# Attention with eight wide products per unit: two bunches of four in place of one per four value products

## Chip, cores and metric

The kernel runs on one core of one Trainium2 chip. The metric is the time of one execution on the device, in microseconds. It is the median of several runs.

## What is computed

Attention (batch 4, 8 heads, 576 positions, head size 64) in float32: heads 0 to 3 see the last 32 positions, heads 4 to 7 every fourth of the last 128. The result, 2304 rows of 512, goes to one of eight experts per row (the arg max of a normalised product with the experts' embeddings), and then through a dense layer pair of 2048 columns. The core of it:

```python
scores = scale * np.matmul(q, k.transpose(0, 1, 3, 2))
scores = np.where(masks[None], scores, -1e9)
attn = np.exp(scores - np.max(scores, axis=-1, keepdims=True))
attn = attn / (np.sum(attn, axis=-1, keepdims=True) + 1e-09)
x = np.matmul(attn, v)                      # attention
expert_idx = np.argmax(logits, axis=1)      # one expert per row
out[mask] = gate_w[mask, None] * (np.maximum(x[mask] @ w1[e], 0) @ w2[e])
h = x @ w_in
return (h - np.tanh(h)) @ w_out
```

## The kernel before

The attention is cut into 19 units. A unit holds 128 query positions in four slots of 64 columns for each of two halves (`par`: partitions 0 to 63 and 64 to 127). Kinds are `d` (dilated heads, with positions four apart brought together), `p` (plain heads) and two for the ends of the sequences (`l`, `t`). Within a unit each group of 32 queries sees 64 keys, so all products of scores and values are small: 64 rows by 32 columns of TensorE's array. They are float32, and each shows in the trace as two records.

The order of the work is written out by hand. The loop over n issues, on each engine in this order:

- loads of later units on SP's queue (`plan[n]`; the first load waits for the copy of pT of the unit before);
- `scores(n + 2)`: two mask products into the score tile `sc` (one buffer, two banks; columns 0 to 255 of each are used), four transposes of keys of unit n + 3, 32 score products' records, four transposes of queries, 32 more (L641, L550, L651);
- `softmax(n + 2)`: on VectorE the maximum (L664) and the difference (L667, which frees `sc`), on ScalarE the exponential (L672);
- `mid[n]`: parts of the routing of earlier rows;
- `values(n)`: into the tile `xo` (one buffer, two banks), 32 value products (64 records, L719), with a wide product of 240 columns ahead of each four products (L717, which calls L631); then four transposes of the probabilities of unit n + 1 (L680), which ScalarE copies to `pT` (L683). VectorE then forms the reciprocal of the sums (L728, L730) and scales (L739, which frees `xo`);
- `after[n]`: copies of values into place (L504, L510, mostly VectorE) and the routing (norm, split, transposes by DMA, choice of expert, scatter of rows to the experts' places by GpSimd).

The wide product, `busy(o)`, multiplies the scaled unit matrix by 16 columns of the mask, repeated, into columns of a bank that nobody reads. It computes nothing that is used. The helper records it at L631.

After unit 16's values the last rows are read back by SP (`load_xt`), a clearing copy writes zeros behind the first expert's rows (`load_first`, L824), and the scatters of the last rows follow on GpSimd. When all rows have been written, the experts begin (L1345), and then the dense layers (L1540, L1596).

Of the kernel before, what the change touches and what calls it, by code (L numbers as in the profile page):

```python
# [56 lines left out]
def kernel(  # L57
# [336 lines left out]
    with ExitStack() as actx:  # L394
# [187 lines left out]
        def run(steps):  # L582
            for f in steps:
                f()
# [6 lines left out]
        def key_window(n, s, g):  # L591
            kind, b, c = units[n]
            if kind == "d":
                return kTd[c][:, s, W * g:W * g + 2 * W]
            if kind == "p":
                o = 256 * c + 128 * (s // 2) + W * g
                return kTp[:, s % 2, o:o + 2 * W]
            if kind == "l":
                return kTl[c][:, g, s, :]
            return kTt[:, s % 2, 2 * (s // 2) + g // 2, W * (g % 2):W * (g % 2) + 2 * W]  # L600

        def value_window(n, s, g):
            kind, b, c = units[n]
            if kind == "d":
                return vwd[b % 2][:, g, c, s, :]
            if kind == "p":
                return vwp[b % 2][:, 4 * (2 * c + s // 2) + g, s % 2, :]
            if kind == "l":
                return vwl[:, g, c, s, :]
            return vwt[:, 2 * (s // 2) + g // 2, g % 2, s % 2, :]  # L610

        def mask_of(n):

            kind, _, c = units[n]
            if kind == "p" and not c:
                return mask_sb[:, :, :]
            e = 0 if kind == "d" else 2
            return mask_sb[:, e].unsqueeze(1).to_broadcast([128, 4, 2 * W])
# [9 lines left out]
        def busy(o):  # L628


            nc.tensor.matmul(  # L631
                o.rearrange("p (r j) -> p r j", j=16), lhsT=idm[:],
                rhs=mask_sb[:, 0, 0:16].unsqueeze(1).to_broadcast([128, o.shape[1] // 16, 16]),
                start=True, stop=True, skip_group_check=True,
            )

        def scores(n, between=(), tag="sc"):
            between = list(between)
            sc = ps.tile([128, 2, 512], F32, tag=tag, name="sc", bufs=1)
            for par in range(2):  # L640
                nc.tensor.matmul(  # L641
                    sc[:, par, 0:256].rearrange("p (r j) -> p r j", r=4), lhsT=idm[:], rhs=mask_of(n),
                    start=True, stop=False, skip_group_check=True,
                )
            half = len(between) // 2
            for par in range(2):
                p0 = 64 * par
                run(between[half * par:half * par + half])
                for s in range(4):
                    for g in range(4):  # L650
                        nc.tensor.matmul(  # L651
                            sc[32 * g:32 * g + 32, par, 64 * s:64 * s + 64],
                            lhsT=qT[n][p0:p0 + 64, s, W * g:W * g + W],
                            rhs=key_window(n, s, g)[p0:p0 + 64],
                            start=False, stop=(s == 3), skip_group_check=True,
                        )
            return sc
# [51 lines left out]
        def values(n, between=()):  # L709
            kind, b, cp = units[n]  # L710
            between = list(between)
            pT = pTs.pop(n)
            xo = ps.tile([128, 2, 512], F32, tag="xo", name="xo", bufs=1)
            for par in range(2):
                p0 = 64 * par
                for s in range(4):
                    busy(xo[:, par, 272:512])  # L717
                    for g in range(4):
                        nc.tensor.matmul(  # L719
                            xo[32 * g:32 * g + 32, par, 66 * s:66 * s + D + 1],  # L720
                            lhsT=pT[p0:p0 + 64, s, 32 * g:32 * g + 32],
                            rhs=value_window(n, s, g)[p0:p0 + 64],
                            start=True, stop=True, skip_group_check=True,
                        )
            run(between)
            xv = xo[:, :, 0:264].rearrange("p a (s d) -> p a s d", d=66)
            rd = wk.tile([128, 2, 4], F32, tag="rd", name="rd")
            nc.vector.tensor_scalar(out=rd, in0=xv[:, :, :, D], scalar1=1e-9, scalar2=None, op0=ALU.add)  # L728
            rr = wk.tile([128, 2, 4], F32, tag="rr", name="rr")
            nc.vector.reciprocal(out=rr, in_=rd)  # L730
            if kind == "p":
                o = xp[b][:, 0, 2 * cp:2 * cp + 2].rearrange("p t (h a d) -> p a (t h) d", h=2, a=2)
            elif kind == "t":
                o = xp[B][:, 0].rearrange("p t (h a d) -> p a (t h) d", h=2, a=2)
            else:
                if cp == 0:
                    xdt[kind, b] = tp.tile([128, 4, 4, D], F32, tag="xd", name="xd")
                o = xdt[kind, b][:, 2 * cp:2 * cp + 2]
            nc.vector.tensor_tensor(  # L739
                out=o, in0=xv[:, :, :, 0:D], in1=rr.unsqueeze(3).to_broadcast([128, 2, 4, D]), op=ALU.mult  # L740
            )
            if kind == "d" and cp == 1:
                (nc.gpsimd if b < 3 else nc.sync).dma_start(out=xd_d[b, 0:128, :], in_=xdt[kind, b].rearrange("p c h d -> p (c h d)"))
            if kind == "l" and cp == 1:
                nc.sync.dma_start(out=xl_d, in_=xdt[kind, b].rearrange("p c h d -> p (c h d)"))
# [409 lines left out]
        init_p()  # L1155
        run(transpose_qk(0))
        softmax(0, scores(0, transpose_qk(1)))
        for g in range(4):
            expand_v(0, g, slice(0, 1))
        softmax(1, scores(1, transpose_qk(2), "xo"))  # L1160
        for g in range(2):
            expand_v(0, g, slice(1, 2))
        mid[0] += [(expand_v, (0, g, slice(1, 2))) for g in range(2, 4)]
        run(transpose_p(0))
        for n in range(N):
            pace["ins"] = done["ins"]
            for f, a in plan[n]:
                f(*a)
            if n + 2 < N:
                softmax(n + 2, scores(n + 2, transpose_qk(n + 3) if n + 3 < N else ()))  # L1170
            for f, a in mid[n]:
                f(*a)
            values(n, transpose_p(n + 1) if n + 1 < N else ())
            for f, a in after[n]:
                f(*a)
            if n == 14:
                dctx.close()
                late.append(actx.enter_context(tc.tile_pool(name="late", bufs=1, side="right")))
# [588 lines left out]
```

## Time and profile before

| | |
|---|---|
| median of three runs | 810.5 us (807.91 to 811.0) |
| profiled execution | 816.94 us, span 815.3 us |
| mean granted clock of TensorE in it | 0.912 |
| TensorE matmul busy | 773.1 us (95%) |
| VectorE busy | 483.1 us (59%) |
| ScalarE busy | 382.0 us (47%) |
| GpSimd busy | 197.9 us (24%) |

The attention lies in the first 182 us of the span, the rest of the routing up to about 209 us, experts and dense layers behind it. PE is TensorE's matmuls, PEld its weight loads, DVE VectorE, ACT ScalarE, POOL GpSimd, SP the engine that issues most DMAs. The granted clock (PEclk) is 1.00 at 2.4 GHz and 0.50 at 1.2 GHz. Matmuls are pipelined, so the time between the starts of two is what one costs, and the busy time of one is longer. A row of the view by windows gives, for a stretch: its length, then the busy time (and count) of PE, PEld, DVE, ACT and POOL, then the granted clock, the busy share of the 16 DMA engines, and GB/s. A row of the timeline gives start, duration, engine, line, operation, output and inputs, shapes, the number of instructions merged, and in brackets the idle time before and what ended it.

### The profile page before, as it was taken

Reading aid. Unit: us, or ns where it says so; the run is one execution under the profiler, and the core shown is the slowest. Engines: PE = TensorE matmul, PEld = TensorE weight load, DVE = VectorE, ACT = ScalarE, POOL = GpSimd, SP = SyncE. Lnnn points to the kernel's source line nnn. Section 1 sums busy time; section 2 is a strip of 40 time slices with the busy share of each in tenths; the row PEclk is TensorE's granted clock in tenths of the full one; section 3 lists DMA queues with packets and bytes.
Section 4 is the critical chain, followed back from the end, with each engine's and each line's share of the span. In section 5 each row is a group of like instructions: output and inputs, shape, how many; then the busy total and the mean of one; then the engine's idle time right before and its main releaser. Section 6 shows DMA issues by size and latency. Waiting matters only on the chain.

```text
span 815.3 us, 16969 instructions
## 1 busy us (share of the span) xinstructions
PE 773.1 (95%) x6773; PEld 470.5 (58%) x6773; DVE 483.1 (59%) x1019; ACT 382.0 (47%) x812; POOL 197.9 (24%) x244
## 2 busy tenths in 40 slices
PE   8999999994799999999999899999999999999994
PEld 4666666562466666688885455555555555555541
DVE  4679465447578777889878999534334343343430
ACT  5446445324365565667765666523423333333401
POOL 2036252407600000000002222322322321321321
PEclk9898575555799999999999999999999999999998
DMA  9768773455898896899840240100100000000001
GB/s 220 164 161 178 119 183 97 84 168 212 260 258 232 244 251 213 203 287 266 283 161 26 29 130 1 39 1 0 39 1 1 29 12 1 17 22 1 9 34 42
DMA packets 115828, 95.33 MB, mean 117 GB/s; under 512 B 72187, under 2 KB 99099, under 8 KB 115739
## 3 DMA queue, kind: packets, MB, share of 16 engines
q1 hardware_dynamic: 109083, 77.12, 35.5%
q0 software_dynamic: 5312, 16.40, 6.1%
q8 instruction: 55, 0.90, 0.5%
q10 hardware_dynamic: 1344, 0.62, 0.3%
q14 instruction: 34, 0.28, 0.1%
HBM read 67.12 MB, written 18.26 MB: 105 GB/s over the span
## 4 chain that ended last, share of the span: by engine, by line
PE 58%; DVE 5%; issue 4%; DMA 3%; ACT 3%; POOL 1%; POOLq 0%; ACTq 0%; SPq 0%; DVEq 0%
PE hp L1540 21%; PE po L1596 19%; PE ph L1345 9%; PE y L1365 8%; DMA wst<-in_moe_w 2%; DVE w2l L187 1%; ACT w2h L177 1%; POOL out L1605 1%; DMA xTe<-xs 1%; DVE hl L1354 1%; DVE y L1424 1%; ACT sq L1403 0%; DVE x2l L1430 0%; POOL gl L1578 0%; ACT u L1550 0%
## 5 line engine op out<-in xcount | busy, mean ns | idle before, releaser
L1553 DVE CUSTOM_DVE_ANT_0 U<-u,sig 128x384 f32<-128x384 f32 x96 | 52.1, 580 | 161.1 <-ACT u L1550 161.1
L1578 POOL TENSOR_TENSOR gl<-c,gh 128x768 f16<-128x768 f32 x48 | 82.5, 1720 | 260.0 <-ACT gh L1577 260.0
L1540 PE MATMUL hp<-x2h,win_h 128*128 128x384 f16 x384 | 125.8, 328 | 4.6 <-DVE c L1560 4.2
L1550 ACT ACTIVATE u<-hp 128x384 f32<-128x384 f32 x96 | 46.0, 485 | 176.1 <-PE hp L1540 170.4
L1540 PE MATMUL hp<-x2h,win_l 128*128 128x384 f16 x384 | 125.8, 328 | 0.0
L1540 PE MATMUL hp<-x2l,win_h 128*128 128x384 f16 x384 | 124.6, 327 | 0.0
L1345 PE MATMUL ph<-xTe,w1h 128*128 128x352 f16 (+6 forms) x512 | 103.4, 296 | 10.9 <-DMA xTe<-xs 8.5
L1540 PEld LDWEIGHTS <-win_h 128*128 128x128 f16 x768 | 75.5, 98 | 58.6 <-DVE c L1560 6.0
L1596 PE MATMUL po<-wo_h,gl 128*128 128x512 f16 x288 | 109.2, 379 | 0.0
L1596 PE MATMUL po<-wo_h,gh 128*128 128x512 f16 x288 | 109.2, 379 | 0.0
L1596 PE MATMUL po<-wo_l,gh 128*128 128x512 f16 x288 | 109.2, 379 | 0.0
L1596 PEld LDWEIGHTS <-gh 128*128 128x128 f16 x576 | 56.3, 98 | 64.5 <-issue 1.0
L1345 PE MATMUL ph<-xTe,w1l 128*128 128x352 f16 (+6 forms) x256 | 75.7, 296 | 0.0
L1365 PE MATMUL y<-hh,w2h 128*128 128x352 f16 (+6 forms) x256 | 74.7, 292 | 0.0
L1365 PE MATMUL y<-hh,w2l 128*128 128x352 f16 (+6 forms) x256 | 74.6, 291 | 0.0
L1365 PE MATMUL y<-hl,w2h 128*128 128x352 f16 (+6 forms) x256 | 74.6, 291 | 0.0
L1345 PEld LDWEIGHTS <-w1h 128*128 128x128 f16 x512 | 50.7, 99 | 26.2 <-issue 9.5
L1365 PEld LDWEIGHTS <-w2h 128*128 128x128 f16 x512 | 50.1, 98 | 17.1 <-issue 0.8
L1540 PEld LDWEIGHTS <-win_l 128*128 128x128 f16 x384 | 37.7, 98 | 26.7 <-issue 0.3
L1582 DVE SCALAR_TENSOR_TENSOR c<-U,c 128x768 f32<-128x768 f32 x48 | 46.0, 958 | 11.2 <-ACT U L1572 11.2
L631 PE MATMUL xo<-mask_sb,idm 128*128 128x240 f16 x152 | 49.6, 326 | 0.0
L1596 PEld LDWEIGHTS <-gl 128*128 128x128 f16 x288 | 28.2, 98 | 34.0
(277 smaller groups left out, 1287.0 us busy)
## 6 DMA issues: line engine op xcount, KB each, us to landing
wst<-in_moe_w SPq DMA_DIRECT2D x64, 512.0 KB, 7.1
wst<-in_moe_w_in SPq DMA_DIRECT2D x16, 512.0 KB, 6.6
wst<-in_moe_w_out SPq DMA_DIRECT2D x16, 512.0 KB, 4.1
vwp<-in_v SPq DMA_DIRECT2D x16, 144.0 KB, 5.2
rv<-in_v SPq DMA_DIRECT2D x4, 512.0 KB, 5.3
rk<-in_k SPq DMA_DIRECT2D x16, 128.0 KB, 4.7
rq<-in_q SPq DMA_DIRECT2D x16, 128.0 KB, 3.3
xp<-xd_d SPq DMA_DIRECT2D x4, 512.0 KB, 5.7
```

Of the source, the lines that this page charges most:

```text
L177: nc.scalar.activation(out=hi, in_=st, func=ACTF.Copy, scale=SW)
L187: nc.vector.scalar_tensor_tensor(out=lo, in0=st, scalar=SW, in1=hi, op0=ALU.mult, op1=ALU.subtract)
L631: nc.tensor.matmul(o.rearrange("p (r j) -> p r j", j=16), lhsT=idm[:], rhs=mask_sb[:, 0, 0:16].unsqueeze(1).to_broadcast([128, o.shape[1] ...
L1345: nc.tensor.matmul(ph[:, 0:CAPS[e]], lhsT=wt[e, f // 2][w][:, c:c + 128], rhs=xT[:, a + d, 0:CAPS[e]], start=(i == 0), stop=(i == 11), ski ...
L1354: rest.append(lambda: nc.vector.scalar_tensor_tensor(out=hl[:, f, c], in0=ph[:, c], scalar=0.0, in1=hh[:, f, c], op0=ALU.max, op1=ALU.subtract
L1365: nc.tensor.matmul(y[dc][:, 0:CAPS[e]], lhsT=w[:, c:c + 128], rhs=h[:, f, 0:CAPS[e]], start=(f == 0 and i == 0), stop=(f == 7 and i == 2), ...
L1540: early(b, "x2", nc.tensor.matmul(hp[:, a, 0:NB], lhsT=w[d][:, 128 * f:128 * f + 128], rhs=x[d][:, c0:c0 + NB], start=(w is win_h and x is ...
L1550: nc.scalar.activation(out=u[:, a], in_=hv[:, a], func=ACTF.Square, accum_out=usum[:, n:n + 1])
L1553: early(b, "sg", nc.vector.tensor_tensor_reduce(out=U[:, a], in0=u[:, a], in1=sig2[:, c0:c0 + NB], scale=1.0, scalar=0.0, op0=ALU.mult, op ...
L1578: nc.gpsimd.tensor_tensor(out=gl, in0=tc_, in1=gh, op=ALU.subtract)
L1582: nc.vector.scalar_tensor_tensor(out=c, in0=U, scalar=T0, in1=c, op0=ALU.add, op1=ALU.mult)
L1596: nc.tensor.matmul(po[t][:], lhsT=g[:, a, 128 * t:128 * t + 128], rhs=w, start=(f == 0 and i == 0), stop=(f == 15 and i == 2), skip_group_ ...
```

## The change

In `scores()` four wide products stand ahead of the two masks, in columns 256 to 495 of the score tile's two banks in turn. In `values()` four stand ahead of all value products, in columns 272 to 511 of `xo`'s two banks in turn, and the one ahead of each four value products is gone. A unit has eight wide products of 240 columns, as before.

```diff
         def scores(n, between=(), tag="sc"):
             between = list(between)
             sc = ps.tile([128, 2, 512], F32, tag=tag, name="sc", bufs=1)
+            for i in range(4):
+                busy(sc[:, i % 2, 256:496])
             for par in range(2):
...
             xo = ps.tile([128, 2, 512], F32, tag="xo", name="xo", bufs=1)
+            for i in range(4):
+                busy(xo[:, i % 2, 272:512])
             for par in range(2):
                 p0 = 64 * par
                 for s in range(4):
-                    busy(xo[:, par, 272:512])
                     for g in range(4):
```

## Rows read from the trace of the kernel before

**Rows 1.** The page: granted clock of TensorE in 40 slices, in tenths.
```profile
PEclk9898575555799999999999999999999999999998
```

**Rows 2.** Windows: the stage of 15 units, then two stretches at the lower clock.
```profile
24.23:157.09 132.86, 131.73 (x2363) 85.86 (x2362) 85.07 (x200) 63.59 (x124) 48.09 (x74) 0.72 0.64 144
...
74.89:112.44 37.55, 37.31 (x548) 24.12 (x548) 20.25 (x58) 16.84 (x33) 16.71 (x26) 0.50 0.81 178
...
132.92:182.00 49.08, 49.08 (x725) 29.95 (x724) 22.73 (x80) 20.04 (x41) 15.58 (x26) 0.50 0.48 127
```

**Rows 3.** Windows of single units; sums of the seven heavy and the eight light.
```profile
32.17:38.81 6.64, 6.64 (x152) 4.45 (x150) 5.11 (x10) 2.93 (x5) 1.74 (x2) 1.00 0.64 181
...
67.67:75.13 7.46, 6.82 (x150) 4.41 (x151) 7.16 (x12) 3.90 (x8) 5.57 (x6) 0.98 1.26 181
...
146.21:157.09 10.88, 10.88 (x151) 6.69 (x150) 5.81 (x20) 4.91 (x11) 1.88 (x5) 0.50 0.45 86
sum 61.51, PE 60.38 PEld 39.69 DVE 46.66 ACT 30.39 POOL 24.47; mean PE 8.63 PEld 5.67 DVE 6.67 ACT 4.34 POOL 3.50
...
sum 71.35, PE 71.35 PEld 46.17 DVE 38.41 ACT 33.19 POOL 23.62; mean PE 8.92 PEld 5.77 DVE 4.80 ACT 4.15 POOL 2.95
```

**Rows 4.** Timeline of TensorE in a unit at the lower clock.
```profile
101.83 1.08 PE L651 MATMUL sc<-kTd,qT 64*32 64x64 f32 x32
102.84 0.38 PE L631 MATMUL xo<-mask_sb,idm 128*128 128x240 f16 x1
103.15 0.44 PE L719 MATMUL xo<-vwd,pT 64*32 64x65 f32 x8
...
108.33 1.12 PE L680 MATMUL pt<-id,pr 128*128 128x128 f32 x4
109.24 0.63 PE L641 MATMUL sc<-mask_sb,idm 128*128 128x256 f16 x2
109.67 1.06 PE L550 MATMUL tr<-id,rk 128*128 128x128 f32 x4
```

**Rows 5.** The same at the upper clock.
```profile
113.19 0.28 PE L631 MATMUL xo<-mask_sb,idm 128*128 128x240 f16 x1
...
116.84 0.66 PE L680 MATMUL pt<-id,pr 128*128 128x128 f32 x4
117.34 0.38 PE L641 MATMUL sc<-mask_sb,idm 128*128 128x256 f16 x2
117.55 0.60 PE L550 MATMUL tr<-id,lk 128*128 128x128 f32 x4
...
119.25 0.65 PE L651 MATMUL sc<-kTp,qT 64*32 64x64 f32 x32
119.83 0.28 PE L631 MATMUL xo<-mask_sb,idm 128*128 128x240 f16 x1
```

**Rows 6.** Groups of instructions in 24.23 to 157.09 us: busy us, mean ns, idle before.
```profile
L950 PE MATMUL rps<-en,xT 128*128 128x8 f16 x96 | 2.9, 169 | 0.0
```

**Rows 7.** Timeline of TensorE around the first values().
```profile
18.84 0.32 PE L719 MATMUL xo<-vwd,pT 64*32 64x65 f32 x8 [0.97 <-ACT pT L683]
...
23.32 1.12 PE L680 MATMUL pt<-id,pr 128*128 128x128 f32 x4
```

**Rows 8.** Timeline of TensorE, SP's queue and GpSimd behind unit 16's scores.
```profile
159.13 0.38 PE L631 MATMUL xo<-mask_sb,idm 128*128 128x240 f16 x1
...
172.47 0.39 SPq L824 DMA_DIRECT2D xs<-z  x1
...
181.32 1.09 POOL L1061 DMA_INDIRECT xs<-xg,ri  x1 [18.81 <-DMA xs<-z]
```

**Rows 9.** The masks' line: its weight loads, ns min/median/max, first and last start.
```profile
L641 PEld LDWEIGHTS <-idm x38: 95/104/152, 6.9 to 157.1; 128*128 128x128 f16 x38
```

**Rows 10.** Windows: the transfers of 20 to 120 us.
```profile
20.00:120.00 100.00, 98.87 (x1837) 64.46 (x1830) 67.55 (x144) 48.26 (x94) 37.46 (x56) 0.76 0.74 161
```

## The prediction

> **What bounds the kernel now.** I began with the page: the granted clock is near full everywhere except in slices 4 to 11, the second part of the attention stage [rows 1]. So I then cut that stage by clock. In 24.2 to 157.1 us the mean granted clock is 0.72: between the two levels, 2.4 and 1.2 GHz, that is 44% of the time at the upper and 56% at the lower, and TensorE is busy for 131.7 of 132.9 us [rows 2]. TensorE's own queue is the limit in this stage, and the level of its clock sets the pace.
>
> Third, the stage by unit. It holds 15 units, each from one pair of masks to the next. A unit wholly at the upper clock takes 6.64 us, one at the lower 10.88 us, and TensorE is busy throughout both [rows 3]. Seven of the units carry so much VectorE work (46.66 us together, 6.7 each) that it would be next: in one of them VectorE is busy for 7.16 of 7.46 us, and TensorE already idle for 0.64. The other eight hold 38.41 us, 4.8 each [rows 3].
>
> Fourth, the inside of a unit on TensorE. At the lower clock a wide product and its four value products (each shows as two records, hence x8) take 0.69 us from wide to wide, and eight such groups 5.49 us, from 102.84 to 108.33. Of that, 0.31 us pass from the start of a wide product to the first value product. But 32 score records of the same small tiles, in an unbroken row, take 1.01 us, and two masks, as wide products as these, 0.43 us [rows 4]. At the upper clock eight groups take 3.65 us, 32 score records 0.58 us and two masks 0.21 us [rows 5]. So eight wide products cost 8 x 0.11 = 0.9 us and 64 small records 2 x 0.58 = 1.2 us when each kind runs in a row, 2.1 us, but 3.65 us when they alternate. The remaining 1.5 us are 16 changes between wide and small tiles.
>
> **What the change does, part by part.** It removes and adds no wide product: eight per unit before and after. It moves four of them out of values() ahead of the masks in scores(), and puts the other four ahead of all value products.
>
> *values(), upper clock.* Four wide products at 0.105 (half a mask pair) are 0.42 us, the one change to small tiles 0.10 (0.31 less 0.21 at the lower clock, taken alike), 64 small records 2 x 0.58 = 1.16: 1.68 us for 3.65. *Lower clock:* 4 x 0.215 + 0.10 + 2 x 1.01 = 2.98 us for 5.49.
>
> *scores().* Four wide products more: 0.42 or 0.86 us. They go ahead of the masks with the same weights, so no change of tile is added. Net, a unit loses 3.65 - 1.68 - 0.42 = 1.55 us at the upper clock and 1.65 us at the lower: 6.64 becomes 5.1 and 10.85 becomes 9.2. This is from both ends: 0, if the alternation is not what costs, to these 1.6 us. I take the upper end, since scores and masks are the nearest rows and have the same shapes.
>
> *Waits.* The first wide product of scores() now waits for the score tile (VectorE's L667 of the unit before), where the mask did; masks, transposes and scores are behind it as before. In the seven heavy units that wait will be there each time, and the 0.42 us come after it; VectorE's own copies (L510, L504) cover them, and without that cover they are in the terms above. In values() the wide products wait for the xo tile only, and run before pT has come. No DMA and no instruction of another engine moves within its queue, on SP and POOL neither.
>
> *What is late next.* With TensorE at 5.1 us, VectorE sets the heavy units: 46.66 x 7.46/7.16 = 48.6 us. The light ones are 8 x 5.1 = 40.8 us. Four units carry the router's small products too (L950 alone 2.9 us, the smaller ones estimated at 0.9, at the lower clock; half at the upper) [rows 6]: 1.9 us. The whole stage at the upper clock would take 91.3 us for 132.9.
>
> *The clock.* Where the level rose, at 112.4 us, TensorE had come through masks, transposes and scores, and the alternating value part followed [rows 2, 4, 5]. The alternation keeps the array waiting at 16 changes per unit, of which the bunches leave two, and the same products then fill less time. That speaks for more of the upper level. Against it, in the heavy units TensorE will stand idle for 1.8 us (6.9 less 5.1) ahead of the scores: the unit with 0.64 us idle ends at 75.1 us, and the level fell at 74.9 [rows 2, 3]. I let half of the seven heavy units fall, and one and a half light ones that follow them before it rises: 5 of 15. They cost 3.5 x (9.2 - 6.9) + 1.5 x (9.2 - 5.1) = 14.2 us more: 91.3 + 14.2 = 105.5, a saving of 27 us. The ends are none low (41.5 us saved) and ten low (seven heavy and three light: 91.3 + 16.1 + 12.3 = 119.7, 13 us saved).
>
> *Start.* The first values() runs from 18.84 to 23.32 us, 4.5 us at a falling clock [rows 7]. Its value products alone are 1.3 us, since its wide products can go before pT is there; less three times 0.42 us ahead of the first scores: 2 us saved (0 to 3).
>
> *Tail.* values(16) begins at 159.13 us at the lower clock; the clearing copy that follows its result through the DRAM copy of the rows is issued at 172.47 and GpSimd waits 18.81 us for it until 181.32, and all scatters that the experts' rows need come behind it [rows 8]. This chain moves as a whole with the end of values(16): 5.49 - 2.98 = 2.5 us (3.8 at the upper clock). values(17) and (18) lie beside it and give nothing.
>
> Sum: 27 + 2 + 2.5 = 31.5 us off the profiled execution's own 816.9 us (span 815.3): **785 us**. The median of the three runs is 810.5, 6.4 us less. If the three had more of the upper clock in this stage, the changed kernel has no further 6 us to gain; if the difference is elsewhere, it is 779. I stay with 785.
>
> On the weight loads, rows and skill differ. Every wide product has its own load of 95 to 104 ns, the masks too, and yet a pair of masks takes 0.21 us at the upper clock and twice that, 0.43, at the lower [rows 4, 5, 9]: the pair's time goes with the clock alone, so the second load is hidden. The Trainium skill ("TensorE: Matmul & The Clock Gate", Part 3, "The mechanism") says that a weight load runs beside a matmul only when their row groups differ, and all wide products have the same. By it, each of the bunch would show its load; that is the first rival below.
>
> **The rivals.**
>
> *1. The wide products of a bunch show their loads.* 8 x 0.096 = 0.77 us per unit, so a unit keeps half its saving. On 16 units 12 us, less what VectorE's work hides in the heavy ones (an estimate: a third): 8 us, 793 us. The spacing of the masks speaks against it. Chance 0.08.
>
> *2. The loads become the bound.* In 20 to 120 us the DMA engines are busy 74% of the time [rows 10]. By the sum above this stretch would take some 78 us (its share of the 27, and the 2 of the start), with the same transfers: 95%. If the engines hold no more than 80% in the mean, it takes 92: 8 us saved, and 8 in the rest of the stage, with the tail 18.5 in all: 798 us. For it: one unit shows 1.26 for its transfers already (more than the engines can hold at once). Against it: TensorE is busy through that stretch, so at today's pace the loads are in time [rows 3, 10]. Chance 0.15.
>
> *3. Slower: the clock stays at the lower level through the whole stage.* Its place is the wait ahead of the scores: one idle time per unit in the heavy ones, and 64 small records with no wide product between them in all. Price: 15 x 9.2 + 3.8 (router's products at that clock) = 141.8 us, 9 more than now, less 2.5 in the tail, and nothing at the start: 823 us. It decides from about 14 of 15 units at the lower clock on; today it is 56%. Against it: the total of TensorE work per unit is the same in less time. The Trainium skill (same page, "A second HAM failure mode") tells of a kernel whose micro-idle times between groups of matmuls made the clock go to and fro; by that rule this rival is the likelier one, and the idle time before 74.9 us agrees with it, while the full use of TensorE in the light units does not. Chance 0.05.
>
> *4. It does not do what it says:* the groups cost the same in a row, and the clock keeps its share: 810 to 817 us. The rows of scores and masks speak against it. Chance 0.05.
>
> **How the numbers follow.** The forecast has 0.67, with its own range of 770 (no low unit: 41.5 + 2 + 3.8 saved) to 799. Range: 768, a little under for the 6 us by which the runs differ, to 803, which takes in rivals 1 and 2 with a margin for both together. Faster by over 0.5% (what a measurement of this kernel can tell from none): forecast and rivals 1 and 2, 0.90; within it 0.05, rival 4; slower 0.05, rival 3.
>
> **What would show it.** In the timeline of TensorE: four wide products 0.1 us (upper) or 0.2 us (lower) apart, then 64 small records in 1.2 or 2.0 us. A unit of 5.1 us at the upper clock in light units, near 7 us in heavy ones, with TensorE idle on L667 before them. Mean granted clock in the stage near 0.83. VectorE's idle time on L728 (value products) gone. GpSimd's wait for the clearing copy, and all behind it, earlier as a whole by the sum. The prediction is wrong if the mean clock falls under 0.72, if TensorE waits on loads by more than 5 us, or if the wide products stand 0.2 us apart at the upper clock.

## The result, and the profile after

The changed kernel takes 787.6 us (median of four runs, 784.61 to 791.65) against 810.75 us (807.91 to 822.64) for the kernel before: a ratio of 0.9729, interval 0.9665 to 0.9793. The forecast was 785 us, from 768 to 803. (Ratios leave disturbed runs of either kernel out, so they can differ a little from the quotient of two medians.) In experiment e9_change_again, on the chip of group 3 below, the ratio is 0.9887, interval 0.9844 to 0.9929: still faster, but by 8 us, since there the kernel before itself takes only 791.38 us. That difference turned out to be half of the story, and is taken up below.

The profiled execution after is one of 786.13 us (span 784.5, mean granted clock 0.948). The page's clock line stands against [rows 1]:

```profile
PEclk9998698658999999999999999999999999999998
```

Of the slices 4 to 11, which were low before, 5 to 8, 10 and 11 are higher; slice 9 still has a 5. The view by windows, for the same stage as [rows 2] and for single units beside those of [rows 3]:

```profile
20.95:132.62 111.67, 94.23 (x2364) 73.21 (x2362) 88.01 (x203) 62.60 (x124) 50.08 (x74) 0.85 0.76 174
...
36.92:41.95 5.03, 5.03 (x152) 3.94 (x150) 3.72 (x8) 3.13 (x6) 0.29 (x1) 1.00 0.71 195
...
48.16:55.07 6.91, 5.27 (x152) 4.08 (x150) 6.62 (x14) 3.78 (x10) 5.66 (x10) 1.00 0.78 136
55.07:62.27 7.20, 5.14 (x152) 4.04 (x150) 6.77 (x14) 5.97 (x13) 5.81 (x7) 1.00 0.21 40
62.27:69.74 7.47, 5.03 (x152) 3.94 (x150) 7.17 (x11) 3.89 (x8) 5.55 (x6) 1.00 1.21 170
69.74:78.84 9.10, 9.10 (x200) 7.33 (x198) 7.42 (x19) 4.78 (x9) 1.98 (x4) 0.55 1.12 315
78.84:87.65 8.81, 8.81 (x161) 6.84 (x159) 5.01 (x20) 5.25 (x12) 2.24 (x4) 0.50 0.67 119
...
116.82:126.92 10.10, 8.17 (x153) 5.84 (x150) 6.74 (x20) 8.80 (x19) 7.90 (x12) 0.75 0.64 223
```

The stage takes 111.67 us, where it took 132.86. The light unit (36.92) takes 5.03 us with TensorE busy throughout; three of the heavy ones (48.16, 55.07, 62.27) take 6.91 to 7.47 us with TensorE busy for only 5.0 to 5.3 and VectorE for 6.6 to 7.2. The heavy unit of 55.07 is no shorter than it was in the kernel before:

```profile
60.48:67.67 7.19, 6.82 (x150) 4.40 (x150) 6.76 (x14) 5.96 (x13) 6.18 (x9) 1.00 0.15 27
```

TensorE is busy for 94 of the stage's 112 us, so it no longer bounds all of it. The light unit of 116.82 took 10.10 us, with 1.9 us of idle time on TensorE, which the prediction did not have.

Inside a unit, the timeline of TensorE against [rows 5], at the upper clock:

```profile
38.84 0.65 PE L653 MATMUL sc<-kTp,qT 64*32 64x64 f32 x32
39.42 0.58 PE L631 MATMUL xo<-mask_sb,idm 128*128 128x240 f16 x4
39.93 1.01 PE L722 MATMUL xo<-vwp,pT 64*32 64x65 f32 x64
40.87 0.65 PE L682 MATMUL pt<-id,pr 128*128 128x128 f32 x4
41.53 0.59 PE L631 MATMUL sc<-mask_sb,idm 128*128 128x240 f16 x4
41.95 0.38 PE L643 MATMUL sc<-mask_sb,idm 128*128 128x256 f16 x2
```

From 39.42 to 40.87 the value part takes 1.45 us (3.65 before, 1.68 predicted). Four wide products ahead of the masks take 0.42 us, from 41.53 to 41.95: 0.105 each, as predicted. At the lower clock the same four take twice that, 0.80 us:

```profile
126.12 1.01 PE L631 MATMUL sc<-mask_sb,idm 128*128 128x240 f16 x4
126.92 0.64 PE L643 MATMUL sc<-mask_sb,idm 128*128 128x256 f16 x2
```

What TensorE waited for in the stage (total us, times, longest), the whole list in the view of waits for 20.95 to 132.62 us. Before, the list of the stage had one line, the score tile's, 1.0 us:

```profile
PE sc L631 <- DVE sm L669: 6.7, 4, 2.4
PE xo L722 <- issue: 4.4, 12, 0.5
PE tr L550 <- DMA rq<-in_q: 2.4, 1, 2.4
PE pt L682 <- issue: 1.6, 2, 1.4
PE xo L631 <- DVE vwp L504: 1.3, 1, 1.3
PE sc L653 <- issue: 0.9, 2, 0.5
```

And the tail, in the order of [rows 8], with the first expert product at the end:

```profile
135.69 0.66 PE L682 MATMUL pt<-id,pr 128*128 128x128 f32 x4
...
143.41 0.39 SPq L827 DMA_DIRECT2D xs<-z  x1
...
152.12 1.09 POOL L1064 DMA_INDIRECT xs<-xg,ri  x1 [12.88 <-DMA xs<-z]
...
179.79 0.45 PE L1348 MATMUL ph<-xTe,w1h 128*128 128x352 f16 x1 [8.31 <-DMA xTe<-xs]
```

values(16) ends at 135.69 us (164.62 before), the clearing copy is issued at 143.41 (172.47), GpSimd goes on at 152.12 (181.32), the first expert product runs at 179.79 (209.2). Each is 29 us earlier: the chain moves as a whole.

### The profile page after: what moved, and what is told of

It reads as the page before. It is cut to its first block, busy times and chain, and to the rows that moved or that the text cites. A ratio compares the mean times of both kernels' runs of the same rounds, so it can differ in the third digit from the quotient of the medians.

```text
span 784.5 us, 16969 instructions
## 1 busy us (share of the span) xinstructions
PE 718.1 (92%) x6773; PEld 451.9 (58%) x6773; DVE 486.3 (62%) x1019; ACT 381.5 (49%) x812; POOL 200.3 (26%) x244
## 4 chain that ended last, share of the span: by engine, by line
PE 63%; DVE 5%; issue 4%; ACT 3%; POOL 1%; DMA 1%; POOLq 0%; SPq 0%; ACTq 0%; DVEq 0%
PE hp L1543 21%; PE po L1599 20%; PE y L1368 11%; PE ph L1348 10%; DVE w2l L187 1%; ACT w2h L177 1%; ACT sq L1406 1%; DVE c L1585 1%; POOL out L1608 1%; DMA xTe<-xs 1%; ACT u L1553 0%; DVE c L1563 0%; ACT U L1575 0%; POOL gl L1581 0%; DVE y L1427 0%
## 5 line engine op out<-in xcount | busy, mean ns | idle before, releaser
L1368 PEld LDWEIGHTS <-w2h 128*128 128x128 f16 x512 | 50.1, 98 | 17.2 <-issue 0.8
L1448 POOL DMA_DIRECT2D row_d<-rw x8 | 4.3, 534 | 174.0 <-ACT rw L1447 174.0
```

Source lines behind the costliest of these rows:

```text
L1368: nc.tensor.matmul(y[dc][:, 0:CAPS[e]], lhsT=w[:, c:c + 128], rhs=h[:, f, 0:CAPS[e]], start=(f == 0 and i == 0), stop=(f == 7 and i == 2), ...
```

## The experiments

Each starts from the changed kernel unless it says otherwise; kernels of one group ran on the same chip with the kernel before.

**Group 1: what the saving is made of.** The kernel before took 812.91 us here.

e1_eight_in_values: all eight wide products in one bunch.

```diff
-            for i in range(4):
-                busy(sc[:, i % 2, 256:496])
...
-            for i in range(4):
+            for i in range(8):
                 busy(xo[:, i % 2, 272:512])
```

> All eight wide products in one bunch ahead of the value products, none ahead of the masks. Theory (the gain is the 16 changes of tile that are gone, and the clock that follows): a unit costs TensorE the same 5.1 us at the upper clock, so the time is that of the change, 785 to 793 us, ratio to the kernel before 0.97. Rival A (the gain comes from the four products ahead of the masks, which fill the part with the scores): 798 us or more, mean granted clock in 21 to 133 us below 0.75.

Measured: 786.28 us (778.12 to 786.85), ratio 0.9707 (0.9569 to 0.9845); stage 110.8 us at a clock of 0.86. The same as the change within its interval: dividing the bunch in two and putting half of it ahead of the masks does not carry the gain.

e2_no_wide: no wide products in the attention. They write columns that nothing reads.

```diff
-            for i in range(4):
-                busy(sc[:, i % 2, 256:496])
...
-            for i in range(4):
-                busy(xo[:, i % 2, 272:512])
```

> All wide products left out; they compute nothing that is used. Theory: the level of the clock hangs on them. A unit would cost TensorE 5.1 - 0.9 = 4.2 us at the upper and 9.2 - 1.8 = 7.4 us at the lower clock, and the stage of 15 units stays at the lower: 15 x 7.4 + 3.8 = 115 us against 112 with the change, so 788 to 795 us, granted clock in the stage below 0.65. Rival B (the wide products are pure cost once the changes of tile are gone): clock 0.8 as with the change, VectorE the bound, 775 to 780 us.

Measured: 784.75 us (784.32 to 785.37), ratio 0.9724 (0.9622 to 0.9825). Both expectations missed: the time is that of the change. Its windows (the stage, a heavy unit, a light one) say why:

```profile
21.37:128.03 106.66, 90.40 (x2244) 72.33 (x2242) 86.26 (x200) 61.38 (x122) 51.71 (x74) 0.67 0.79 180
...
53.76:60.95 7.19, 6.78 (x142) 5.30 (x142) 6.76 (x14) 5.96 (x13) 6.20 (x9) 0.50 0.06 9
...
76.57:83.39 6.82, 6.82 (x157) 5.69 (x155) 4.41 (x23) 3.42 (x9) 0.73 (x2) 0.50 0.90 177
```

The clock falls to 0.67 (0.85 with the wide products), but a heavy unit takes 7.19 us at 0.50, as it does at 1.00 in the change (7.20) and in the kernel before (7.19). TensorE is busy in it for 6.78, 5.14 and 6.82 us, VectorE for 6.76 or 6.77 in all three: VectorE sets it at either level. The light unit that took 8.81 us at the lower clock with the products (78.84 above) takes 6.82 us without. The equal times then mean that what the clock takes is about what the wide products cost; that balance is read from these rows and not measured by itself.

e3_small_changes_back: the change, plus one product of only 16 columns ahead of each four value products. Little work returns, but all 16 changes of tile do.

```diff
                 for s in range(4):
+                    busy(xo[:, par, 272:288])
                     for g in range(4):
```

> The change, and beside it a product of 16 columns ahead of each four value products: the changes of tile are back, with a fifteenth of the columns. Theory: eight groups take 8 x (0.456 - 0.1) = 2.8 us at the upper clock where 64 records in a row took 0.95, so a unit costs 6.8 us again and the time comes near the kernel before: 803 to 813 us. Rival A (what counts is where the wide columns stand): 8 x 16 columns are 0.05 us per unit, 787 to 790 us.

Measured: 810.04 us (803.27 to 818.25, ten runs), ratio 0.9983 (0.9925 to 1.004): all of the gain is gone, while the stage (131.95 us) keeps a clock of 0.79, above the 0.72 of before.

```profile
61.20 0.18 PE L631 MATMUL xo<-mask_sb,idm 128*128 128x16 f16 x1
61.31 0.32 PE L723 MATMUL xo<-vwp,pT 64*32 64x65 f32 x8
61.56 0.18 PE L631 MATMUL xo<-mask_sb,idm 128*128 128x16 f16 x1
```

The timeline shows it at the upper clock: a group takes 0.36 us from wide to wide, eight of them 2.9 us, while the 64 value records in a row take 0.94 (39.93 to 40.87 above). The difference is 1.9 us. By its columns, a product of 16 is a fifteenth of one of 240, which takes 0.105 us: 0.06 us for all eight. Each also loads its own 128x128 weights, but the load is not the price either: in the profile of the change the router's 48 products of 8 columns, each with such a load, stand 0.025 us apart when they run in a row at the upper clock:

```profile
110.13 1.35 PE L953 MATMUL rps<-en,xT 128*128 128x8 f16 x48
111.35 0.57 PE L631 MATMUL sc<-mask_sb,idm 128*128 128x240 f16 x4
```

Eight of them make 0.2 of the 1.9 us. The rest, about 1.7 us, goes with the changes of tile. This is the run that decides: alternating the tiles cost the time, whatever the wide products compute. What a change of tile spends its time on is not shown by any run.

e5_wide_waits_for_nothing: the four of scores() go to a bank of their own, ahead of the score tile.

```diff
+        rbank = ps.tile([128, 512], F32, name="rps", bufs=1)
+        rps = rbank[:, 0:80].rearrange("p (a t e) -> p a t e", a=2, t=5)
...
-            sc = ps.tile([128, 2, 512], F32, tag=tag, name="sc", bufs=1)
             for i in range(4):
-                busy(sc[:, i % 2, 256:496])
+                busy(rbank[:, 272:512])
+            sc = ps.tile([128, 2, 512], F32, tag=tag, name="sc", bufs=1)
...
-        rps = ps.tile([128, 2, 5, E], F32, name="rps", bufs=1)
```

> The four wide products of scores() write free columns of the bank of the routing's tile, so they no longer wait for VectorE's L669 (the change's line of the difference that frees the score tile) and fill part of the idle time ahead of it. Theory: per heavy unit up to 0.42 us less between that wait and the scores, mostly hidden by VectorE, and a clock that falls less often: granted clock in the stage 0.85 to 0.95 for 0.83, 778 to 788 us. Rival C (the falls of the clock come from TensorE's gaps among the value products, not from that wait): no difference, 785 to 791 us.

Measured: 791.74 us (791.31 to 793.33), ratio 0.9812 (0.9708 to 0.9917): above both expected ranges. It decides nothing, because the edit brought a wait of its own: the wide products now wait for VectorE's reads of the routing tile that shares the bank, and the wait for the score tile stays.

```profile
PE rps L631 <- DVE base L1050: 4.0, 2, 3.3
PE sc L646 <- DVE sm L672: 3.6, 2, 2.2
PE rps L631 <- DVE lo L970: 2.3, 2, 1.5
```

**Group 2: what still holds the stage.** The kernel before took 805.56 us on this chip.

e4_sixteen_wide: eight and eight (both `range(4)` become `range(8)`).

> Eight wide products in each bunch in place of four, 16 per unit. Theory (the columns cost TensorE's time and buy clock, and the two about cancel, as the kernel without wide products had 0.67 of the clock in the stage and the same time): a light unit 5.9 us at the upper clock, heavy units as before at 7; 8 x 0.84 = 7 us more in the light units, less what fewer falls of the clock give back (34 us at the lower clock in the stage, at most 12 us to gain): 784 to 795 us, clock in the stage above 0.88. Rival B (the clock is worth more than the columns): below 782 us.

Measured: 786.81 us (784.27 to 789.05), ratio 0.9809 (0.9719 to 0.9898); stage 111.2 us, clock 0.92. More of the upper clock, bought with as much work: no gain.

e6_scatters_later: the unit of 116.82 in the profile after has a series of short idle times of TensorE for which the profile names nothing ("issue"):

```profile
119.83 0.41 PE L722 MATMUL xo<-vwp,pT 64*32 64x65 f32 x11
120.46 0.32 PE L722 MATMUL xo<-vwp,pT 64*32 64x65 f32 x4 [0.21 <-issue]
121.22 0.32 PE L722 MATMUL xo<-vwp,pT 64*32 64x65 f32 x5 [0.45 <-issue]
121.95 0.44 PE L722 MATMUL xo<-vwp,pT 64*32 64x65 f32 x4 [0.40 <-issue]
```

They lay beside GpSimd's scatters, in both units that have some, so the scatters were moved to later units.

```diff
-            after[4 * b + 9].append((route_place, (b,)))
+            after[4 * b + 9].append((lambda g: turns(route_rank(g)), (b,)))
+            after[(11, 14)[b]].append((route_scatter, (b,)))
```

> The change, with GpSimd's eight scatters of the first two routing groups issued two units and one unit later (after unit 11 and 14 in place of 9 and 13). In the profile of the change TensorE runs value products in groups of about ten instructions per 0.6 us, waiting for nothing that shows, at 91 to 97 and 120 to 124 us, when these scatters run. Theory S (the scatters slow TensorE's supply of instructions): the two series move to where the scatters are now, units at the old places take 5 to 7 us and not 10. Rival F (something at that place of the program): the series stay at scores and values of units 9 and 13. Time 783 to 792 us in either case.

Measured: 788.19 us (780.97 to 791.73), ratio 0.9824 (0.9714 to 0.9934). The series is gone from its old place, here in a row of the windows, a unit of 5.48 us (87.65 in the change: 10.40):

```profile
86.28:91.76 5.48, 5.04 (x153) 3.94 (x150) 5.14 (x14) 3.28 (x8) 3.99 (x7) 1.00 0.78 122
```

Nor does it appear where the scatters now are: in the timeline of GpSimd a scatter, and in that of TensorE the value products behind it, in one unbroken row.

```profile
97.79 1.06 POOL L1064 DMA_INDIRECT xs<-xg,ri  x1 [0.31 <-issue]
...
104.04 1.56 PE L722 MATMUL xo<-vwd,pT 64*32 64x65 f32 x64
```

This does not clear the scatters, because e4, e7 and e9, with the scatters where they were, have no such series either. The profiles of e1, e2, e3 and e5, all taken on the chip of group 1, have it again, each time at the scatters or just behind them; those of e4 and of e6 to e12, on the two other chips, do not have it at all. So the scatters alone do not bring it, something of the chip or of the execution belongs to it, and e6 was measured on a chip on which no profile shows it. Its cause stays open.

e7_more_copies_on_scalar: every second copy of V goes to ScalarE, not every third (`VP = 3` becomes `VP = 2`).

> The change, with every second copy of values (L510) on ScalarE, not every third. VectorE loses a quarter of its L510 time, some 6 us over the stage, and ScalarE gets 10 copies of 0.6 us. Theory (VectorE sets the heavy units of 7 us): the heavy units get 0.5 to 1 us shorter, stage 107 to 109 us for 111.7, 782 to 786 us. Rival C (TensorE or the loads set them): no difference, 785 to 791 us.

Measured: 782.4 us (781.63 to 784.8), ratio 0.9761 (0.9678 to 0.9845). In the stage's window VectorE is busy for 79.8 us, where it was 88.0, and the stage is 6 us shorter at the same clock, more than the 3 to 5 us expected:

```profile
23.30:128.71 105.41, 90.01 (x2365) 71.64 (x2362) 79.77 (x188) 67.84 (x131) 48.25 (x74) 0.86 0.79 177
```

Not all of the 6 us is VectorE's work. The stage begins 2.35 us later than in the change (23.30 for 20.95), and this profile has no series of "issue" gaps. Against e9, the change again and without the series too, the stage ends 2.0 us earlier (128.71 for 130.75). The clean comparison is e10 with e11 below, on one chip: the same step, without wide products, takes 779.91 us for 783.86, and their times do not overlap. Work taken from VectorE saves time, as it should where VectorE sets the heavy units.

e8_no_wide_more_on_scalar: e2 and e7 together.

> No wide product, and every second copy of values on ScalarE. Theory: without wide products TensorE at the lower clock (7.4 us per unit) sets most units, so less work on VectorE gives less than it does to the change: 781 to 785 us. Rival B (VectorE sets the units there too): 777 to 780 us.

Measured: 780.37 us (779.47 to 784.23), ratio 0.9735 (0.9651 to 0.9819); stage 106.2 us, clock 0.72. It lies between the two expectations and decides for neither.

**Group 3: the best of them beside the change.** The kernel before took 791.38 us on this chip.

e9_change_again (no edit), e10_no_wide_more_on_scalar_again (e8) and e11_no_wide_again (e2):

> The change itself once more, beside the next three on one chip. 784 to 790 us. Theory on the gaps of TensorE at 91 to 97 and 120 to 124 us: if they hang on the program they come again at scores and values of units 9 and 13; if on the chip or on what was loaded before, they may be absent, as in the kernel with the scatters later.

> No wide product, every second copy of values on ScalarE, again. Theory (VectorE and the loads set the units once TensorE is under 5 us at the upper and 7.4 us at the lower clock): 779 to 784 us, 3 to 8 us under the change in the same call. Rival (the wide products are needed for the clock): as slow as the change or slower.

> No wide product, again. Theory (columns and clock cancel): 783 to 788 us, within 4 us of the change in the same call, with a granted clock in the stage of 0.65 to 0.72.

e12_no_wide_two_thirds_on_scalar: e2, with two of three V copies on ScalarE.

```diff
-            (nc.scalar.copy if ncopy[0] % VP == 0 else nc.vector.tensor_copy)(out=o, in_=i)
+            (nc.scalar.copy if ncopy[0] % 3 != 0 else nc.vector.tensor_copy)(out=o, in_=i)
```

> No wide product, two of three copies of values on ScalarE. Theory: VectorE loses half of its L510 time, some 13 us over the stage, ScalarE gets 20 copies of 0.6 us and is at 6 us in some heavy units; TensorE at the lower clock (7.4 us) is then the bound: 776 to 783 us. Rival (ScalarE's order delays the copies of pT and queries): 783 us or more.

| kernel | median, us | ratio to before | interval |
|---|---|---|---|
| e9 | 783.44 (780.38 to 787.99) | 0.9887 | 0.9844 to 0.9929 |
| e10 | 779.91 (778.23 to 782.47) | 0.985 | 0.9812 to 0.9888 |
| e11 | 783.86 (782.94 to 785.62) | 0.9898 | 0.9861 to 0.9935 |
| e12 | 780.12 (777.86 to 783.53) | 0.9846 | 0.9805 to 0.9887 |

e9 came out just under its expected range, the other three within theirs. Without any wide product the time is again that of the change (e11, e9). With half of the V copies on ScalarE it is 3.5 us less (e10); two thirds of them there give nothing beyond that (e12). The versions that beat both kernels are e10 and e12, by medians; the intervals of e10 and e9 still overlap a little.

## Why the prediction was right

**The cost of alternating tiles: right, and shown.** A light unit at the upper clock takes 5.03 us (predicted 5.1), one at the lower 8.81 with some router products in it (predicted 9.2), three heavy ones at the upper 6.9 to 7.5 (predicted 6.9). e3 brings back the changes of tile, with next to no work, and loses the whole gain. The Trainium skill ("TensorEngine Tiling (Array Packing)", Tiling Modes, "Key Properties") says that a change of tiling mode drains TensorE, and gives no price. That it is a drain no run here shows; what a pair of changes costs they do show, about 0.24 us at the upper clock in e3 (0.36 us per group, less 0.94/8 for its small records), with the product of 16 columns in it.

**The stage: right in sign, too large.** It fell by 21.2 us, not 27, and two terms of the sum were off against each other. The first is idle time of TensorE. The sum has it for VectorE's score work alone, and there it fits: 6.3 us (1.8 in each of 3.5 heavy units), measured 6.7. All other waits stand in it at nothing, and they came to 10.6 us: 6.9 us of "issue", 2.4 us for a load, 1.3 us for the copy of V. Nearly all of them lie in the light units, which took 61.6 us together where the sum has 40.8 at the upper clock; the heavy ones took 50.1 for 48.6. The second is the clock. Five units of 9.2 us at the lower level are 46 us, and would make a mean clock of 0.78 in a stage of 105.5 us, not the 0.83 that the prediction names. The measured 0.85 is 34 us at the lower level, so part of the missing idle time was paid back here. The waits are seen in the trace; no run took them away one by one. The series of "issue" gaps alone is not the difference: e9's stage, without it but with longer waits for DMAs, is hardly shorter.

```profile
20.67:130.75 110.08, 93.77 (x2364) 73.86 (x2362) 85.83 (x203) 62.79 (x124) 50.42 (x74) 0.81 0.79 177
```

**The start and the tail: too small.** The masks of unit 3 come 3.3 us earlier (predicted 2). From the masks of unit 18 to the end of values(16) now pass 3.07 us for 7.53: 4.5 us (predicted 2.5), since the clock there is now at the upper level. The three terms make 29.0 us at the end of values(16), and 30.8 at the end of the span, for the 31.5 forecast: the errors cancelled in part, and that is luck. By the medians the saving is 23 us; the forecast came near the time because it took the 31.5 us off one execution that was 6 us over the median.

**Where half of the gain comes from.** Each run lists its mean granted clock and its span; the time at the lower level is 2 x (1 - clock) x span. Over the 23 runs of the kernel before, on three chips, that the ratios of groups 1 to 3 rest on, the span is 760.3 us plus 0.40 for each us at the lower level, with a standard deviation of 2.0 us (at most 3.6): from 787.0 us at a clock of 0.957 (68 us low) to 811.2 at 0.921 (128 low). The rows of the light units give nearly that factor, 1 - 6.64/10.88 = 0.39 [rows 3]. The ten runs of the change have a mean span of 783.8 us with 87 us low; the kernel before would take 795.0 us with as much. So, as an estimate, about 11 us of the gain are there at an equal clock (10 to 15 by the flatter lines through the runs of one chip each), close to eight light units at 1.55 us = 12.4; heavy ones give little, as VectorE sets them. The rest is time at the lower level that the kernel before has more of, and that goes with the chip and the execution: 116 us low in the mean on the chip of group 1, 77 on that of group 3, where the gain is 8 us. On that chip the change itself is no less at the lower level (87 us in the mean of e9), so the step that the bunches bring more of the upper clock did not hold there. The prediction took one profiled execution's 0.72 in the stage for the kernel's own. It said what was at stake in this (6 us of difference to the median), and the time fell near; but it did not see that 788 to 823 us all belong to the kernel before.

**The rivals.** *1, the weight loads show:* fell. Four wide products stand 0.105 us apart at the upper clock, each with a load of about 0.1 us [rows 9], which is therefore hidden. The rule of the Trainium skill that the prediction names ("TensorE: Matmul & The Clock Gate", Part 3, "The mechanism") is not borne out for these products of equal row groups; the same section also lets a load go ahead into a background buffer, and that this trace does not contradict. *2, the loads become the bound:* did not happen; TensorE waited 2.4 us for a load, at a DMA share of 0.76. In e9 it waited 3.3 us for loads and 3.7 us for a transpose by DMA in the routing, at 0.79; the two together pass the 5 us that the prediction gave as a sign of being wrong, and its median was 783.44 us all the same. *3, the clock stays low:* fell, since the stage's mean rose to 0.85. But its mechanism shows. All four falls of the level in the changed stage lie in idle time of TensorE or at most 1.5 us behind it, as the granted clock of these windows tells (33.2, 70.7, 94.6 and 121.9 us):

```profile
33.00:34.00 1.00, 1.00 (x19) 0.44 (x8) 0.69 (x1) 0.23 (x1) 0.00 (x0) 0.59 1.26 140
70.00:71.00 1.00, 1.00 (x34) 0.83 (x35) 0.95 (x3) 0.97 (x2) 0.00 (x0) 0.86 1.24 396
94.00:95.00 1.00, 0.49 (x5) 0.28 (x5) 0.00 (x0) 0.09 (x1) 0.88 (x2) 0.81 0.91 207
121.00:122.00 1.00, 0.38 (x7) 0.24 (x9) 0.26 (x1) 0.97 (x2) 0.95 (x3) 0.96 0.60 85
```

The first two stand behind these waits, for a load and for the score tile; the other two are inside the series of "issue" gaps.

```profile
31.68 0.93 PE L550 MATMUL tr<-id,rq 128*128 128x128 f32 x4 [2.40 <-DMA rq<-in_q]
...
69.32 0.58 PE L631 MATMUL sc<-mask_sb,idm 128*128 128x240 f16 x4 [2.44 <-DVE sm L669]
```

The rule of the Trainium skill on micro-idle times ("TensorE: Matmul & The Clock Gate", "A second HAM failure mode"), which the prediction names, agrees with these four falls. But it does not say which idle time brings one: the other three waits for the score tile (1.06, 1.14 and 2.06 us) brought none, and in the kernel before three falls (44.2, 122.7, 132.9 us) came with TensorE busy throughout, one of them in this window:

```profile
122.00:123.00 1.00, 1.00 (x26) 0.55 (x21) 0.62 (x1) 0.34 (x1) 0.00 (x0) 0.84 0.99 344
```

My own step, that half of the heavy units would fall because of their idle time, is right for one of the four waits (70.7 us). The other three falls came from idle time that the sum did not have, so that the mean of 0.85 lies near the 0.83 is luck. *4, nothing happens:* excluded by the interval.

**The waits.** VectorE's reads of the score tile hold up the first wide product in heavy units, as said: 6.7 us in four waits. That this wait costs nothing by itself is not shown: e5 was to tell, and did not.

## What to carry to other kernels

Products of different tile shapes should run in bunches: look in TensorE's timeline for short groups of alternating shapes, and compare the time per group with an unbroken row of either kind. Work that only keeps a clock up has to be weighed against no such work at all: here none, eight and sixteen wide products per unit gave the same time once they were bunched, at clocks of 0.67, 0.85 and 0.92 in the stage (none and eight side by side on one chip: 783.86 and 783.44 us). Before the clock's share of a gain is counted on, the kernel before should be seen on more than one chip, as a plot of span against clock.

## What had not been expected of the hardware

- The time of one kernel on one core goes with its mean granted clock along one line, and the clock differs between chips and executions: 77 us at the lower level in the mean on one chip, 116 on another (23 runs).
- A heavy unit takes 7.2 us at either level of the clock (7.20 at 1.00, 7.19 at 0.50 in e2), and took as much before the change (7.19 at 1.00).
- Products of 8 columns on the whole array, each with its own weights, stand 0.025 us apart in a row at the upper clock; a product of 16 columns between groups of small tiles adds 0.24 us.
- In some executions TensorE issues some 4 to 11 records and then stands for 0.2 to 0.45 us, with no wait that the profile shows; two units of the changed kernel took over 10 us with this series in them. It is there again in e1, e2, e3 and e5, all on one chip and beside the scatters, and absent in e4 and e6 to e12 on two others. The cause is open.
